# Expert 0's gathers: free of the last head group's stores, and taken head group by head group

## The chip, the cores and the metric

The kernel runs on one core of a Trainium2 chip. Its time is device microseconds (us) of one launch. The core's engines are named as the profile names them: PE multiplies matrices and also transposes them, DVE and ACT do elementwise work, POOL is a second elementwise engine that also issues the indirect transfers (gathers and scatters), and SP only issues plain transfers. Each engine takes its own instructions strictly in order; an instruction that has to wait holds up everything behind it on its engine. The transfers themselves run on 16 DMA engines shared by all issuers.

## What is computed

```python
# threshold attention: B=8, H=8, S=576, D=64
scores = q @ k.T / sqrt(D)
scores = where(scores >= max(scores) - tau, scores, -1e9)
attn   = softmax(scores)
x      = (attn @ v), laid out as 4608 tokens x 512      # a token's 8 heads side by side
# hash routing: E=8 experts, F=1024
e      = token_ids * 2654435761 % 8                       # depends on the ids alone
out[t] = relu(x[t] @ w1[e]) @ w2[e]
```

## The kernel before

**Attention.** The 64 (batch, head) problems are taken as 32 pairs: two neighbouring heads of one batch item. Pair `p` has `hp, b = divmod(p, 8)`, so the first eight pairs are head group 0 of all eight batch items, the next eight are group 1, and pairs 24 to 31 are group 3, the last. A head group is 128 columns of `x`. The loop runs over steps `n`, five to a pair (`p, s = divmod(n, 5)`), in an order of instructions that is written out by hand for every engine. In a step, PE makes scores (L235), DVE negates them and takes their maximum (L246, tile `ns`), POOL makes the threshold from the maximum (L253, tile `thr`), ACT exponentiates (L260), DVE applies the threshold to the exponentials (`mask`, L271, needs `thr`); two steps later PE transposes the weights (L282), ACT copies them (L303) and PE multiplies them with `v` (L313). The scores of a pair's first step are the only ones with a 64 row tile (`64*64` in the profile), so they mark where a pair begins.

**x goes through DRAM.** Two pairs late, in step `s == 0`, `put_xm` scales pair `p - 2`'s result (DVE, L352, tile `xm`) and SP stores it: one transfer of 256 KB (L358) and two of 16 KB (L363) into `x_scratch`, 576 rows of one head group's 128 columns. SP's queue also carries, in the same order as written, the loads of `k` (L190 to L192), `q` (L187) and `v` (L208, L212) for coming pairs, and four loads of 2 MB for the weights of the first two experts (L134 in pairs 20 and 24, L140 in pairs 22 and 26).

**Routing and expert 0's gathers.** Which tokens go to which expert is worked out during the first 23 pairs. Expert 0's tokens (up to 5 tiles of 128, `kt` = 0 to 4) are then fetched from `x_scratch` while the attention still runs: one gather is 128 rows of one head group (`fetch_0(kt, hp)`, issued on POOL by L119, into columns `128 hp` of buffer `xg_kt`). The 15 gathers of head groups 0 to 2 are spread over the last pairs; they stand in POOL's order between the `thr` instructions. The five of head group 3 follow after the loop, when pair 31 has been stored. Both sides name the whole of `x_scratch` to the scheduler of dependences: a gather names rows by an index, so it is taken to read all of it.

```python
 # L681  G0 = NS * ((HP - 1) * B + 1)                                    (= 125, the start of pair 25)
 # L682  early = [(kt, hp) for kt in range(KT) for hp in range(HP - 1)]
 # in the loop over n, in this order:
 s == 0: load_pair(p + 2), load_v(p + 1)        # SP: k, q, v
 s == 2, p in (22, 26): load_w2(...)            # SP: 2 MB
 s == 1: scale_k(p + 1)                         # POOL, L215
 s == 0, p >= 2: put_xm(p - 2)                  # DVE L352, SP L358, L363
 every s: mask(n - 1, j)                        # DVE L271
 if s in (2, 3) or s == 4 and n < G0 + 2 * NS:
     fetch_early(n)                             # POOL L119: next of `early`, if n > G0
```

So pairs 25 and 26 have three gathers each (s = 2, 3, 4), pairs 27 to 30 two (s = 2, 3), and the fifteenth is at n = 157 in pair 31.

**After the loop's last pair.** At n = 160 PE transposes what was gathered of tiles 0 to 3 (L614, 24 transposes) and, a little later, of tile 4; ACT copies the result into `xT_0`, and PE runs three quarters of expert 0's first layer (L640) while the last pairs finish. The experts follow in order of their load.

Of the kernel before, what the change touches and what calls it, by code (L numbers as in the profile page):

```python
# [20 lines left out]
def kernel(  # L21
# [12 lines left out]
    nc = tc.nc  # L34

    B, H, D, S = qT.shape
    N, DIN = out.shape
    E, _, F = w1.shape
    P = 128
    HP = H // 2  # L40
# [7 lines left out]
    NQ = 4  # L48
    TAIL = NQ * P
    NC = 5  # L50
    NS = 5
# [5 lines left out]
    KT, NB = 5, 19  # L57
# [21 lines left out]
    x_dram = nc.dram_tensor("x_scratch", (N, DIN), FP32, kind="Internal").ap()  # L79
    x_rows = x_dram.rearrange("n (h d) -> (n h) d", h=HP)  # L80
# [25 lines left out]
    gidx_0 = consts.tile([P, KT, HP], I32, name="gidx_0")  # L106
# [6 lines left out]
    xg_bufs = [consts.tile([P, DIN], FP32, name=f"xg_{i}") for i in range(KT)]  # L113
# [2 lines left out]
    w_tiles = {}  # L116

    def gather(src, dst, idx):
        nc.gpsimd.indirect_dma_start(  # L119
            out=dst, out_offset=None, in_=src,  # L120
            in_offset=bass.IndirectOffsetOnAxis(ap=idx, axis=0),
            bounds_check=src.shape[0] - 1, oob_is_err=False)

    def fetch_0(kt, hp):
        gather(x_rows, xg_bufs[kt][:, P * hp:P * hp + P], gidx_0[:, kt, hp:hp + 1])

    def expert_at(e):

# [15 lines left out]
    with tc.tile_pool(name="a_q", bufs=1) as a_q, \  # L144
# [59 lines left out]
        def load_v(p):  # L204
            hp, b = divmod(p, B)
            v_sb = v_bufs[p % 3]
            rows = v[b].rearrange("s h d -> s (h d)")[:, hp * P:hp * P + P]
            nc.sync.dma_start(out=v_sb[:, 0:4],  # L208
                              in_=rows[0:TAIL].rearrange("(c p) m -> p c m", p=P))
            for j in range(2):  # L210
                half = slice(64 * j, 64 * j + 64)
                nc.sync.dma_start(out=v_sb[half, 4, half], in_=rows[TAIL:S, half])  # L212
# [121 lines left out]
        def x_place(p):  # L334
            hp, b = divmod(p, B)
            return b * S, hp * P
# [10 lines left out]
        def put_xm(p):  # L347


            rec = recs.pop(p)  # L350
            xm = a_x.tile([P, NS, P], FP32, name="xm")
            nc.vector.tensor_tensor(  # L352
                out=xm[:].rearrange("p t (j d) -> p t j d", j=2),
                in0=av[:, :, 0:NS * D].rearrange("p j (t d) -> p t j d", t=NS),
                in1=rec[:].rearrange("p (t j) -> p t j", j=2)[:, :, :, None]
                .to_broadcast([P, NS, 2, D]), op=ALU.mult)
            r0, c0 = x_place(p)
            nc.sync.dma_start(  # L358
                out=x_dram[r0:r0 + TAIL, c0:c0 + P].rearrange("(t p) m -> p t m", p=P),
                in_=xm[:, 0:NQ])  # L360
            for j in range(2):
                cols = slice(D * j, D * j + D)
                nc.sync.dma_start(out=x_dram[r0 + TAIL:r0 + S, c0 + D * j:c0 + D * j + D],  # L363
                                  in_=xm[64 * j:64 * j + 64, NQ, cols])

        def route():

# [171 lines left out]
        def scatters():  # L539
# [20 lines left out]
            for _ in range(4):  # L560
# [11 lines left out]
                          in_=bass.AP(tensor=dataclasses.replace(token_ids.tensor,  # L572
                                                                 shape=[2 * N], dtype=I32),
                                      offset=0, ap=[[2 * NTC, P], [2, NTC], [1, 2]]))
# [94 lines left out]

        LAST = NS * NP  # L670
        G0 = NS * ((HP - 1) * B + 1)
        early = [(kt, hp) for kt in range(KT) for hp in range(HP - 1)]
        pieces, scatter_pieces = route(), scatters()
        h_pieces, held, LATE = early_h(), {}, (0, 6, 1, 7, 2, 3, 4, 5)
        assert FO == 8
# [12 lines left out]
        with tc.manual_schedule():  # L688
# [3 lines left out]
            for _ in range(17):  # L692
                nc.tensor.transpose(tr[:, 0, 0:P], ident[:], ident[:])
            nc.gpsimd.dma_start(out=tau_in[:],
                                in_=bass.AP(tensor=tau.tensor, offset=0, ap=[[0, P], [1, 1]]))
# [14 lines left out]
            for n in range(LAST + NS + 1):  # L710
                p, s = divmod(n, NS)
                m = n - 2
                if s == 0 and p + 2 < NP:
                    load_pair(p + 2)
                if s == 0 and p + 1 < NP:
                    load_v(p + 1)
                if s == 2 and p in (20, 24):
                    load_w1(p // 4 - 5)
                if s == 2 and p in (22, 26):
                    load_w2((p - 22) // 4)  # L720

                if (s == 3 and p > 0 or s == 2 and p in (9, 11, 13)) and not placed:
                    next(pieces)
                if s == 1 and 3 <= p < 2 + KT:
                    nc.sync.dma_start(out=xg_bufs[p - 2][:], in_=xg_bufs[0][:])

                if s == 1 and 2 + KT <= p < 2 + KT + N // DIN:
                    r0 = DIN * (p - 2 - KT)
                    nc.sync.dma_start(
                        out=x_dram[r0:r0 + DIN, DIN - P:].rearrange("(t p) m -> p t m", p=P),  # L730
                        in_=xg_bufs[0][:].rearrange("p (t m) -> p t m", m=P))
                q = p - 1
                if s == 1 and 0 <= q < NP:
                    add_eps(q)
                if s == (1 if p else 3) and p + 1 < NP:
                    scale_k(p + 1)
                if s == 2 and 0 <= q < NP:
                    nc.vector.reciprocal(recs[q][:], recs[q][:])
                if n == LAST + NS:
                    fill(2)  # L740
                if s == 0 and p >= 2:
                    turn_o()
                if n == LAST:
                    for k in (0, 2):
                        tr = ps_sc.tile([P, 2, 512], FP32, name="sc")
                        early_xT(tr, k, k + 2, 0, CO - 1)
                if s in (1, 2) and 0 <= q < NP and n != LAST + 1:
                    av_part(q, 0, ((0, 1, 2), (3, 4))[s - 1])
                if n < LAST and s in (1, 2):
                    negate(n, 0)  # L750
                    expo(n, 0)
                if s == 2 and 0 <= q < NP:
                    put_oT(0)
                if n > LAST:
                    fill(1)
                turned = 0 <= m < LAST
                if turned:
                    tr = turn_w(m, 0)
                    put_wT(m, 0, tr)
                if n == LAST:  # L760
                    put_xm(p - 2)
                    av_part(q, 0, (0, 1, 2))
                if n >= LAST:
                    fill(1)
                if n == LAST:
                    tr = ps_sc.tile([P, 2, 512], FP32, name="sc")
                    early_xT(tr, 4, 5, 0, CO - 1)
                if s in (3, 4) and 0 <= q < NP:
                    av_part(q, 1, ((0, 1, 2), (3, 4))[s - 3])
                if n < LAST and s not in (1, 2):  # L770
                    negate(n, 0)
                    expo(n, 0)
                if s == 0 and p > 0 and not placed:
                    next(pieces)
                if s == 0 and p >= 2 and n != LAST:
                    put_xm(p - 2)
                if s == 4 and 0 <= q < NP:
                    put_oT(1)
                if s in (3, 4) and turned:
                    tr = turn_w(m, 1)  # L780
                if n + 1 < LAST:
                    score(n + 1, 0)
                if s == 4 and turned:
                    put_wT(m, 1, tr)
                if n < LAST and heads(n) == 2:
                    negate(n, 1)
                    expo(n, 1)
                if s == 3 and turned:
                    put_wT(m, 1, tr)
                if n + 1 < LAST:  # L790
                    score(n + 1, 1)
                if s in (0, 1) and turned:
                    tr = turn_w(m, 1)
                    put_wT(m, 1, tr)
                if 0 < n <= LAST:
                    for j in range(heads(n - 1)):
                        mask(n - 1, j)
                if s < NS - 1 and placed:
                    next(scatter_pieces, None)
                if s in (2, 3) or s == 4 and n < G0 + 2 * NS:  # L800
                    fetch_early(n)
                if n == LAST:
                    fill(1)
            assert not early
            nc.vector.tensor_tensor(out=stok[:], in0=stok[:], in1=stok_odd[:], op=ALU.min)
            for h in range(4):
                rows, n = slice(32 * h, 32 * h + 32), (NB - h + 3) // 4
# [3 lines left out]
            for g in range(4):  # L811
                rows, n = slice(32 * g, 32 * g + 32), min(KT, NB - KT * g)
                nc.vector.tensor_copy(gidx_x[rows, 1:, 0:n], stok[rows, 1:, KT * g:KT * g + n])
            for _ in pieces:
                pass
            nc.vector.scalar_tensor_tensor(
                out=qidx[:], in0=stok[:], scalar=4.0,
# [7 lines left out]
    with tc.tile_pool(name="m_x", bufs=1) as m_x, \  # L825
# [534 lines left out]
        with tc.For_i(0, n_ov, 1) as it:  # L1360
# [5 lines left out]
                out=w1_sb[:],  # L1366
                in_=w1[bass.ds(ex, 1)].rearrange("o (c p) f -> p (o c) f", p=P))
            nc.gpsimd.dma_start(
                out=w2_sb[:],
                in_=w2[bass.ds(ex, 1)].rearrange("o (c p) d -> p (o c) d", p=P))  # L1370
# [53 lines left out]
```

## Time and profile before

| | us |
|---|---|
| median of 3 runs | 919.86 |
| lowest and highest of them | 915.38 and 920.58 |
| the profiled execution's own time | 919.78 |
| its span, first to last instruction | 918.1 |
| PE busy | 902.2 (98%) |
| DVE busy | 757.1 (82%) |
| POOL busy | 500.6 (55%) |
| granted TensorE clock | 0.998 |

A row of a timeline gives the start, the duration, the engine, the line and operation, what it writes and reads, and in square brackets the time that the engine was idle before it and what ended that idle time. `SPq` is SP's queue; its rows are the issuing of a transfer, not the transfer itself.

### The profile page before, as it was taken

To read this page: it belongs to the slowest core of one execution; us is meant where nothing else is said; L and a number is where in the kernel's file an instruction comes from. 1 tells how busy PE (TensorE), PEld (TensorE's weight loads), DVE (VectorE), ACT (ScalarE), POOL (GpSimd) and SP (SyncE) were. 2 spreads that over 40 slices of the span, in tenths; PEclk is the share of its full clock that TensorE was granted. 3 is DMA by queue.
4 is the path that set the end of the run, shared out by engine and by line. 5 is a ranking of instruction groups with operands and counts; after the bars stand their busy time and mean duration, and the time that the engine had idled before them with its cause. 6 is when DMAs were issued, how large, how long until landed. Compare 5 with 4: busy or idle time off the path is not lost.

```text
span 918.1 us, 21471 instructions
## 1 busy us (share of the span) xinstructions
PE 902.2 (98%) x7663; PEld 669.2 (73%) x7663; DVE 757.1 (82%) x1711; ACT 514.0 (56%) x848; POOL 500.6 (55%) x703
## 2 busy tenths in 40 slices
PE   8999999999999999999999999999999999999996
PEld 5666666666666666556668989889898988979885
DVE  8999999999999999989945796868778687776831
ACT  6888888888888898788922141422314132141321
POOL 4433443457667633545414388693959769391752
PEclk9999999999999999999999999999999999999999
DMA  7364463554546668654011546354343635431101
GB/s 179 92 148 119 111 153 96 136 127 109 126 95 142 182 165 223 186 125 104 16 30 53 159 167 211 118 165 156 85 159 130 208 115 151 157 91 30 32 23 55
DMA packets 114779, 113.15 MB, mean 123 GB/s; under 512 B 32475, under 2 KB 89315, under 8 KB 114672
## 3 DMA queue, kind: packets, MB, share of 16 engines
q1 hardware_dynamic: 105168, 92.64, 38.3%
q0 software_dynamic: 9072, 18.91, 6.6%
q8 instruction: 62, 1.02, 0.5%
q14 instruction: 45, 0.37, 0.1%
q10 hardware_dynamic: 432, 0.21, 0.1%
HBM read 81.99 MB, written 21.44 MB: 113 GB/s over the span
## 4 chain that ended last, share of the span: by engine, by line
PE 48%; POOL 27%; issue 15%; DVE 3%; ACT 2%; SPq 1%; DMA 1%; POOLq 1%; DVEq 0%; ACTq 0%
PE av L313 17%; POOL out_dram L1247 17%; PE sc L235 15%; PE tr L282 11%; POOL stok_odd L1232 8%; POOL xg L119 3%; PE sc L640 3%; PE av L282 2%; ACT w L260 1%; SPq L1277 1%; DVE w L271 1%; ACT wT_a L303 1%; DVE ns L246 1%; DMA k_sb<-in_k_dram 1%; POOLq L1247 0%
## 5 line engine op out<-in xcount | busy, mean ns | idle before, releaser
L260 ACT ACTIVATE w<-ns,nmx 128x576 f32<-128x576 f32 x288 | 220.3, 776 | 32.4 <-DVE ns L246 31.9
L271 DVE SCALAR_TENSOR_TENSOR w<-ns,thr,w 128x576 f32<-128x576 f32 x288 | 226.2, 817 | 4.2 <-POOL thr L253 4.2
L246 DVE TENSOR_SCALAR_CACHE_REDUCE ns<-sc 128x576 f32<-128x576 f32 x288 | 205.3, 745 | 6.7 <-PE sc L235 6.1
L1247 POOL DMA_INDIRECT out_dram<-o_q,qidx x127 | 147.7, 1163 | 113.4 <-DVE o_q L1238 80.1
L253 POOL TENSOR_SCALAR thr<-nmx,drop 128x2 f32<-128x2 f32 (+1 forms) x160 | 100.7, 630 | 165.8 <-DVE ns L246 157.8
L235 PE MATMUL sc<-k_sb,q 64*128 64x288 f32 (+1 forms) x1280 | 179.0, 422 | 1.4 <-DVE ns L246 1.0
L282 PEld LDWEIGHTS tr<-ident,w 64*128 64x128 f32 x2624 | 106.3, 138 | 92.5 <-ACT wT_a L303 28.8
L282 PE MATMUL tr<-ident,w 64*128 64x64 f32 x2624 | 138.9, 230 | 5.5 <-ACT wT_a L303 2.9
L235 PEld LDWEIGHTS sc<-k_sb,q 64*128 64x128 f32 (+1 forms) x1280 | 92.1, 177 | 24.8 <-DVE ns L246 12.2
L313 PE MATMUL av<-wT_a,v 128*64 128x320 f32 (+1 forms) x704 | 100.4, 418 | 0.2
L303 ACT COPY wT_a<-tr 128x512 f32<-128x512 f32 (+1 forms) x128 | 81.6, 638 | 22.4 <-PE tr L282 21.9
L303 ACT COPY wT_b<-tr 128x512 f32<-128x512 f32 (+1 forms) x128 | 81.2, 634 | 9.8 <-PE tr L282 8.1
L313 PE MATMUL av<-wT_b,v 128*64 128x256 f32 x640 | 83.2, 389 | 0.0
L1232 POOL COPY stok_odd<-stok 128x152 int32<-128x152 int32 x157 | 71.4, 455 | 0.6
L313 PEld LDWEIGHTS av<-wT_a,v 128*64 128x64 f32 x704 | 43.7, 136 | 29.0 <-DVE xm L352 0.5
L937 PE MATMUL bank<-h,w_sb 128*128 128x288 f32 (+4 forms) x248 | 62.0, 402 | 0.0
L937 PEld LDWEIGHTS bank<-h,w_sb 128*128 128x128 f32 x248 | 58.7, 290 | 0.5
L937 PE MATMUL sc<-h_s,w_s 128*128 128x288 f32 (+2 forms) x224 | 56.6, 406 | 0.0
L313 PEld LDWEIGHTS av<-wT_b,v 128*64 128x64 f32 x640 | 40.2, 136 | 18.8 <-issue 0.7
L961 ACT ACTIVATE h<-h 128x576 f32<-128x576 f32 (+1 forms) x42 | 29.0, 692 | 41.4 <-DVE h L864 36.3
L542 POOL DMA_INDIRECT slot_scratch<-tok,slot_i x36 | 46.6, 1294 | 8.5 <-issue 8.3
L119 POOL DMA_INDIRECT xg<-x_scratch,gidx_x x35 | 43.9, 1255 | 12.3 <-DVE xq L1269 5.3
(241 smaller groups left out, 1383.2 us busy)
## 6 DMA issues: line engine op xcount, KB each, us to landing
w_sb<-in_moe_w_dram SPq DMA_DIRECT2D x16, 2048.0 KB
q<-in_q_dram SPq DMA_DIRECT2D x62, 288.0 KB
v<-in_v_dram SPq DMA_DIRECT2D x32, 256.0 KB
x_scratch<-xm SPq DMA_DIRECT2D x32, 256.0 KB
xT<-xq SPq DMA_DIRECT2D x84, 80.0 KB
k_sb<-in_k_dram SPq DMA_DIRECT2D x31, 144.0 KB
k_sb<-in_k_dram SPq DMA_DIRECT2D x32, 112.0 KB
x_scratch<-xg SPq DMA_DIRECT2D x9, 256.0 KB
```

What stands on the lines that cost most here:

```text
L119: nc.gpsimd.indirect_dma_start(out=dst, out_offset=None, in_=src, in_offset=bass.IndirectOffsetOnAxis(ap=idx, axis=0), bounds_check=src.sh ...
L235: nc.tensor.matmul(sc[out_rows, i, 0:S2], lhsT=q_sb[rows, h, q0:q1], rhs=k_sb[rows, h], start=True, stop=True)
L246: nc.vector.tensor_scalar(out=ns[:].rearrange("p (i s) -> p i s", i=2), in0=sc[:, :, 0:S2], scalar1=-1.0, scalar2=None, op0=ALU.mult, op1= ...
L253: nc.gpsimd.tensor_scalar(out=thr[:, 0:j + 1], in0=stats[n][0][:, 0:j + 1], scalar1=drop[:], scalar2=None, op0=ALU.add)
L260: nc.scalar.activation(w, nss[n, j][:], AF.Exp, bias=stats[n][0][:, j:j + 1], scale=-1.0)
L271: nc.vector.scalar_tensor_tensor(out=w, in0=nss.pop((n, j))[:], scalar=stats[n][1][:, j:j + 1], in1=w, op0=ALU.is_le, op1=ALU.mult, accum_ ...
L282: nc.tensor.transpose(dst[:, r, 64 * c:64 * c + 64], src[rows, c0:c0 + P], ident[rows, rows])
L303: nc.scalar.copy(dst, tr[:, :, 0:64 * n_c].rearrange("p r (c q) -> p r c q", c=n_c))
L313: nc.tensor.matmul(av[64 * j:64 * j + 64, g, c0:c1], lhsT=v_sb[:, c, 64 * j:64 * j + 64], rhs=wT[g][:, i, c0:c1], start=(c == 0), stop=stop)
L937: nc.tensor.matmul(ps[:, i], lhsT=lhsT, rhs=y[:, c], start=start and c == 0, stop=c == len(lhsTs) - 1, skip_group_check=not start)
L1232: nc.gpsimd.tensor_copy(stok_odd[:], stok[:])
L1247: inst = nc.gpsimd.indirect_dma_start(out=rows[:, :], out_offset=bass.IndirectOffsetOnAxis(ap=idx, axis=0), in_=o_sb, in_offset=None, boun ...
```

## The change

It does three things. Stores of head group 3 and gathers of head groups 0 to 2 are declared to have no dependence on each other, which is so because they touch different columns; the gathers still depend on the stores of groups 0 to 2. The list of gathers is turned round: all five tiles of head group 0, then of group 1, then of group 2, instead of three groups of one tile after the other. And pair 26 has two gathers instead of three: the only one left at s = 4 is n = 129.

```diff
     def gather(src, dst, idx):
-        nc.gpsimd.indirect_dma_start(
+        return nc.gpsimd.indirect_dma_start(
...
+    def other_dims(inst, own, others):
+        inst = getattr(inst, "ins", inst)
+        tc.declare_no_dep(inst, group=others,
+                          reason="the last head pairs' dims are stored, dims of earlier ones gathered")
+        tc.add_to_no_dep_group(own, inst)
+
     def fetch_0(kt, hp):
-        gather(x_rows, xg_bufs[kt][:, P * hp:P * hp + P], gidx_0[:, kt, hp:hp + 1])
+        inst = gather(x_rows, xg_bufs[kt][:, P * hp:P * hp + P], gidx_0[:, kt, hp:hp + 1])
+        if hp < HP - 1:
+            other_dims(inst, "gathers", "stores")
...
             r0, c0 = x_place(p)
-            nc.sync.dma_start(
+            stores = [nc.sync.dma_start(
                 out=x_dram[r0:r0 + TAIL, c0:c0 + P].rearrange("(t p) m -> p t m", p=P),
-                in_=xm[:, 0:NQ])
+                in_=xm[:, 0:NQ])]
             for j in range(2):
                 cols = slice(D * j, D * j + D)
-                nc.sync.dma_start(out=x_dram[r0 + TAIL:r0 + S, c0 + D * j:c0 + D * j + D],
-                                  in_=xm[64 * j:64 * j + 64, NQ, cols])
+                stores.append(nc.sync.dma_start(
+                    out=x_dram[r0 + TAIL:r0 + S, c0 + D * j:c0 + D * j + D],
+                    in_=xm[64 * j:64 * j + 64, NQ, cols]))
+            if c0 == P * (HP - 1):
+                for inst in stores:
+                    other_dims(inst, "stores", "gathers")
...
-        early = [(kt, hp) for kt in range(KT) for hp in range(HP - 1)]
+        early = [(kt, hp) for hp in range(HP - 1) for kt in range(KT)]
...
-                if s in (2, 3) or s == 4 and n < G0 + 2 * NS:
+                if s in (2, 3) or n == G0 + 4:
                     fetch_early(n)
```

## The prediction

> **What bounds the kernel now.** I start with the page's first part, for which engine has no time to spare.
>
> ```profile
> span 918.1 us, 21471 instructions
> PE 902.2 (98%) x7663; PEld 669.2 (73%) x7663; DVE 757.1 (82%) x1711; ACT 514.0 (56%) x848; POOL 500.6 (55%) x703
> ```
>
> PE is busy nearly all the time, and the change takes no work from it. So a gain can come only from places where PE is made to wait or runs late, and only in the stretch that has the gathers. The timeline of PE shows that stretch, one row per pair: the first scores of pairs 26 to 31.
>
> ```profile
> 370.13 0.71 PE L235 MATMUL sc<-k_sb,q 64*64 64x288 f32 x8
> ...
> 384.46 0.71 PE L235 MATMUL sc<-k_sb,q 64*64 64x288 f32 x8
> ...
> 399.69 0.71 PE L235 MATMUL sc<-k_sb,q 64*64 64x288 f32 x8
> ...
> 416.20 0.72 PE L235 MATMUL sc<-k_sb,q 64*64 64x288 f32 x8
> ...
> 430.08 0.71 PE L235 MATMUL sc<-k_sb,q 64*64 64x288 f32 x8
> ...
> 443.98 0.71 PE L235 MATMUL sc<-k_sb,q 64*64 64x288 f32 x8
> ```
>
> The differences are 14.33, 15.23, 16.51, 13.88 and 13.90. Pair 25, which begins at 356.24, takes 13.89 too, so 13.89 is what a pair costs undisturbed, and pairs 26, 27 and 28 are 0.44, 1.34 and 2.62 too long: 4.40 us in all. Everything that this change can win is in there. DVE's timeline in the same stretch says what made them long.
>
> ```profile
> 369.88 0.82 DVE L271 SCALAR_TENSOR_TENSOR w<-ns,thr,w 128x576 f32<-128x576 f32 x1 [0.41 <-POOL thr L253]
> ...
> 385.04 0.82 DVE L271 SCALAR_TENSOR_TENSOR w<-ns,thr,w 128x576 f32<-128x576 f32 x1 [1.24 <-POOL thr L253]
> ...
> 401.61 0.82 DVE L271 SCALAR_TENSOR_TENSOR w<-ns,thr,w 128x576 f32<-128x576 f32 x1 [2.59 <-POOL thr L253]
> ```
>
> Three masks wait for their threshold, 4.24 us together, against 4.40 on PE: 0.41 answers to 0.44, 1.24 to 1.34, 2.59 to 2.62. POOL's timeline says why the thresholds were late: a gather stood in front of each.
>
> ```profile
> 368.36 1.13 POOL L119 DMA_INDIRECT xg<-x_scratch,gidx  x1 [3.94 <-DVE w L271]
> ...
> 383.56 1.10 POOL L119 DMA_INDIRECT xg<-x_scratch,gidx  x1 [4.82 <-DVE ns L246]
> ...
> 400.12 1.10 POOL L119 DMA_INDIRECT xg<-x_scratch,gidx  x1 [6.21 <-DMA x_scratch<-xm]
> ...
> 411.77 1.10 POOL L119 DMA_INDIRECT xg<-x_scratch,gidx  x1 [1.29 <-DMA x_scratch<-xm]
> ```
>
> The DVE named in the first two had long been done; all four wait for the newest store of x to land. Idle time on POOL minus the loss on DVE is 3.53, 3.58 and 3.62: a gather may hold POOL up for 3.6 us for nothing, since a threshold is ready that long before its mask, and every microsecond more is lost on DVE and PE. The fourth, 1.29, costs nothing, as it must. Last, SP's waits and its timeline show that the store was late in its turn.
>
> ```profile
> SPq L358 <- DMA xg<-x_scratch,gidx: 30.6, 5, 11.0
> ```
> ```profile
> 378.17 0.37 SPq L358 DMA_DIRECT2D x_scratch<-xm  x1
> ...
> 396.54 0.37 SPq L358 DMA_DIRECT2D x_scratch<-xm  x1
> ```
>
> Pair 24's result is ready on DVE at 372.86 and SP has issued the loads before it at 374.90, but the store goes at 378.17, when the third gather (begun 372.15) has landed. Pair 25's could go at 391.97 and goes at 396.54. Gather waits for store, store waits for gather, and both pass through busy DMA engines: a 2 MB load of w2 is issued at 380.60.
>
> **The change, part by part.** *The waits between gathers and group 3's stores go.* The first gather (n = 127) comes before any store of group 3: the last store ahead of it is pair 23's, of group 2, issued at 361.54. It still waits for that one, 3.94 us, so 0.41 on DVE and 0.44 on PE stay. The waits of 4.82, 6.21 and 1.29 are for stores of pairs 24, 25 and 26, all of group 3, and go: DVE gains 1.24 + 2.59 = 3.83, and PE, by its pairs, 1.34 + 2.62 = 3.96. What is late next in those pairs? Pairs 29 and 30 have two gathers each at the same places in POOL's order, and waited for no store; they take 13.88 and 13.90. So I put pairs 27 and 28 at 13.89.
>
> *SP no longer waits for gathers to land*: the stores of pairs 24, 25 and 26 leave earlier, pair 24's by 3.3 us (374.90 for 378.17), the other two by up to some 8, and so does what is queued behind them. The 2 MB load of w2 moves from 380.60 to about 377.4. The next loads of k (382.87) are no earlier, because they wait for PE to free their buffer; they run behind w2 as now. Nobody waits for w2 before the experts. I cost this at nothing; the cover is time: a load of k is issued some 18 us before POOL scales it (382.87 and 406.78 minus the 4 gained for pair 29's), and w2, issued at 380.60, had let SP's queue go on at 391.97. Were that cover gone, POOL would hold back a threshold, and PE lose one for one beyond 3.6.
>
> *A wait is added*: the scaling of k (L215), which sits on POOL ahead of the next threshold, now names its own three loads, which a gather's wait for later stores had covered. Queued behind it are `thr`, then the masks. It is the wait that the scalings of the earlier pairs have; the 31 scalings together idled 2.8 us, 0.09 each. Below nothing is excluded, since it is an added wait; above, five at 0.09 are 0.5, if all of it came out on PE. They have 3.6 us of cover, so I take 0.
>
> *The order of the gathers and the one moved.* POOL issues 15 gathers before and after, 1.0 to 1.65 each, all on POOL between thresholds. The gather at n = 134 goes, and one at n = 158 comes. There POOL has this room (timeline of POOL, around the last gather):
>
> ```profile
> 452.31 1.39 POOL L119 DMA_INDIRECT xg<-x_scratch,gidx  x1 [0.16 <-issue]
> 454.27 0.71 POOL L253 TENSOR_SCALAR thr<-nmx,drop 128x2 f32<-128x2 f32 x1 [0.57 <-DVE ns L246]
> 457.37 0.72 POOL L253 TENSOR_SCALAR thr<-nmx,drop 128x2 f32<-128x2 f32 x1 [2.38 <-DVE ns L246]
> ```
>
> A gather of 1.4 us goes into the idle 2.38 with 0.8 to spare: nothing. But the last gathers are needed sooner after their issue. Tile 3's last one moves to 452.3 and tile 4's to about 455.1, and PE takes them in here:
>
> ```profile
> 458.50 0.91 PE L614 MATMUL sc<-ident,xg 64*128 64x64 f32 x24
> ...
> 462.06 0.37 PE L614 MATMUL sc<-ident,xg 32*128 32x32 f32 x3
> ```
>
> That leaves 6.2 and 7.0 us from issue to use. The slowest landing that the stretch shows, from a gather's start to the store it let go, is 9.2 us (387.35 to 396.54), beside w2's load; another took 6.4 (401.75 to 408.19). At 452 SP's timeline has no load under way, and the last five gathers of the kernel, issued into the same quiet at 478.69 to 485.06, are all used by 489.16, the very last within 4.1. Cost 0 at 4.1; at the other end 9.2, a stall of 3.0. I take 0, by the nearer row.
>
> *Sum*, against the profiled execution: 919.78 - 3.96 = 915.8, of it 918.1 - 3.96 = 914.1 span. After 404 PE runs without a gap worth naming, and the experts' gathers and loads start from events on PE's path, so the gain should reach the end undiminished. The profiled execution and the median of the runs shown (919.86) are the same to 0.1, so 915.8 holds for the median as well. It is 0.43%. About 1% is what a measurement of this kernel can tell from no change: the three runs of before alone lie 5.2 us apart, so this forecast counts as within 1%.
>
> **A rule weighed against the rows.** The Trainium skill, "DMA: Bandwidth & Descriptors", section "Anatomy of one DMA — SWDGE (gpsimd) path", gives a transfer issued from GpSimd a nearly constant 2.0 us plus bytes over 436 GB/s. A gather of 64 KB would land about 2.2 us after its issue. By that, pair 24's store would leave at 375.4, pair 25's as soon as SP is free, 391.97, and with the landing times of the stores in the trace (5.4 and 3.6) the gathers behind them would wait about 2.0 and 1.7, under the 3.6 that are free: the removed waits would be worth nothing, and the time 919.8. The rows say 6.0 and 9.2 us from gather to released store, and a loss on DVE; they decide. Where the DMA engines are quieter than in this execution, though, the rule's case comes nearer, which is why my range leans upwards.
>
> **Rivals.** *The gain is partly there already or partly given back.* The run of 915.38 lies 4.4 below the others, the same 4.4 that these pairs lose; if the loss comes and goes with the state of the DMA queues, its removal moves the median less. Or a pair with gathers and freely moving stores costs more than 13.89: pairs 13 to 21, in which POOL issues the routing's scatters at the same places, take 13.89 to 14.47 by the same view of PE. At 0.4 each for the five pairs with moved gathers, 2 us come back: 917.8. Against it speak pairs 29 and 30. *More goes*: the first wait falls under its 3.6 too, 0.44 more, and the median falls on the low side of the scatter: 911 to 910. No row offers more. *Slower: the late gathers.* The transposes at n = 160 wait for the last gathers of tiles 3 and 4, PE stops, and all behind stop with it. Up to 6.2 us from issue it costs nothing, from there one for one, and it outweighs the gain from 6.2 + 4.0 = 10.2 us on; at 13 us the stall would be 6.8 and the time 919.8 - 4.0 + 6.8 = 922.6. Nothing in the trace landed that late. That the change *does not do what it says* I can exclude nearly: in the order of instructions with their waits, the stores of group 3 lose their waits for gathers, and gathers 4 to 15 theirs for stores.
>
> **Chances.** Forecast, 914 to 916.5: 0.64. Part given back, 916.5 to 920.5: 0.18. More, down to 911 and below: 0.10. Slower, above 920.5, through late gathers or a queue that I misjudge: 0.08. Range 911.0 to 920.5, which leaves out the last two. Faster by over 1% needs less than 910.7 (0.10); slower by over 1% needs more than 929.1, which takes gathers that land 20 us after issue or something unseen (0.05); within 1% the rest (0.85).
>
> **What would show it.** Right: pair 26 still 14.3, pairs 27 and 28 at 13.9; on POOL one gather with an idle time near 4 and no other above 1; the stores of pairs 24 and 25 right behind the loads of v; w2 issued near 377; the 24 transposes of L614 without a wait. Wrong: a mask that still waits for `thr` by more than 0.5 us after 371, a scaling of k with idle time before it, or a gap on PE at the first L614; and a pair of 14.3 among 27 to 31 would mean that a gather beside free stores has a price that I set to nothing.

## The result and the profile after

| | before | after |
|---|---|---|
| median of 13 runs each, us | 919.23 | 914.05 |
| lowest to highest | 915.38 to 921.04 | 913.57 to 914.76 |
| the profiled execution's own time | 919.78 | 914.5 |
| its span | 918.1 | 912.9 |

The measured ratio is 0.9964, with a 95% interval of 0.9952 to 0.9976, so 3.3 us (2.2 to 4.4). It is not the plain quotient of the two medians above, which lie 5.2 apart (0.9944); in the first group of experiments below, where both kernels ran on one chip, the medians lie 3.5 apart (917.27 and 913.78). The forecast was 915.8, a ratio of 0.9957. The second thing in the table is as large as the first: the runs of before are spread over 5.7 us, those of after over 1.2.

The page of after begins with these two lines; in the lines of after, the code lines are 8 or 12 higher than in before (L235 is now L243, L358 is L366).

```profile
span 912.9 us, 21463 instructions
...
PE 900.5 (99%) x7663; PEld 669.8 (73%) x7663; DVE 758.2 (83%) x1711; ACT 514.0 (56%) x848; POOL 503.3 (55%) x703
```

The same instructions on PE, less time. PE's timeline, the first scores of pairs 25 to 29:

```profile
355.25 0.72 PE L243 MATMUL sc<-k_sb,q 64*64 64x288 f32 x8
...
369.13 0.71 PE L243 MATMUL sc<-k_sb,q 64*64 64x288 f32 x8
...
383.03 0.72 PE L243 MATMUL sc<-k_sb,q 64*64 64x288 f32 x8
...
397.07 0.71 PE L243 MATMUL sc<-k_sb,q 64*64 64x288 f32 x8
...
410.96 0.71 PE L243 MATMUL sc<-k_sb,q 64*64 64x288 f32 x8
```

Pairs 25 to 28 take 13.88, 13.90, 14.04 and 13.89, where before had 13.89, 14.33, 15.23 and 16.51: 55.71 for 59.96, a gain of 4.25. From pair 29 to the end of the span both executions take the same, 501.90 and 501.94, so nothing is given back. The rest of the 5.2 us between the two spans, 0.99, lies before pair 25, where the instructions are the same; more on it below. POOL's timeline has the gathers of pairs 25 to 28, here the first of each pair:

```profile
365.98 1.13 POOL L119 DMA_INDIRECT xg<-x_scratch,gidx  x1 [2.56 <-DVE ns L254]
...
377.47 1.39 POOL L119 DMA_INDIRECT xg<-x_scratch,gidx  x1 [0.16 <-issue]
...
391.36 1.39 POOL L119 DMA_INDIRECT xg<-x_scratch,gidx  x1 [0.16 <-issue]
...
405.41 1.39 POOL L119 DMA_INDIRECT xg<-x_scratch,gidx  x1 [0.16 <-issue]
```

Only the first still waits. SP's timeline has the stores of pairs 24 and 25 and the load of w2 between them:

```profile
373.96 0.38 SPq L366 DMA_DIRECT2D x_scratch<-xm  x1
...
376.43 0.40 SPq L148 DMA_DIRECT2D w_sb<-in_moe_w_dram  x1
...
389.18 0.49 SPq L366 DMA_DIRECT2D x_scratch<-xm  x1
```

All three go 4 to 7 us earlier than before (1 us of it from ahead of pair 25), as soon as SP has issued what is ahead of them. And the list of DVE's waits from 355 to 460 us, which before was headed by 4.2 us of masks waiting for `thr`, has no mask left in it:

```profile
DVE ns L254 <- PE sc L243: 1.4, 7, 0.3
DVE rec L750 <- POOL rec L351: 0.7, 1, 0.7
```

### The profile page after: what moved, and what is told of

The parts are those of the page before. It is cut to its first block, busy times and chain, and to the rows that moved or that the text cites. A ratio compares the mean times of both kernels' runs of the same rounds, so it can differ in the third digit from the quotient of the medians.

```text
span 912.9 us, 21463 instructions
## 1 busy us (share of the span) xinstructions
PE 900.5 (99%) x7663; PEld 669.8 (73%) x7663; DVE 758.2 (83%) x1711; ACT 514.0 (56%) x848; POOL 503.3 (55%) x703
## 4 chain that ended last, share of the span: by engine, by line
PE 49%; POOL 28%; issue 15%; DVE 3%; ACT 2%; SPq 1%; DMA 1%; POOLq 1%; DVEq 0%; ACTq 0%
PE av L321 18%; POOL out_dram L1259 17%; PE sc L243 15%; PE tr L290 10%; POOL stok_odd L1244 7%; POOL xg L119 4%; PE sc L652 3%; PE av L290 1%; SPq L1289 1%; ACT w L268 1%; DMA k_sb<-in_k_dram 1%; DVE w L279 1%; DVE ns L254 1%; POOLq L1259 0%; PE sc L949 0%
## 5 line engine op out<-in xcount | busy, mean ns | idle before, releaser
L261 POOL TENSOR_SCALAR thr<-nmx,drop 128x2 f32<-128x2 f32 (+1 forms) x160 | 103.5, 647 | 169.3 <-DVE ns L254 163.9
L243 PE MATMUL sc<-k_sb,q 64*128 64x288 f32 (+1 forms) x1280 | 178.6, 423 | 1.0 <-DVE drop L716 0.7
L243 PEld LDWEIGHTS sc<-k_sb,q 64*128 64x128 f32 (+1 forms) x1280 | 92.8, 177 | 22.8 <-DVE ns L254 9.6
```

Source lines behind the costliest of these rows:

```text
L243: nc.tensor.matmul(sc[out_rows, i, 0:S2], lhsT=q_sb[rows, h, q0:q1], rhs=k_sb[rows, h], start=True, stop=True)
L261: nc.gpsimd.tensor_scalar(out=thr[:, 0:j + 1], in0=stats[n][0][:, 0:j + 1], scalar1=drop[:], scalar2=None, op0=ALU.add)
```

## Experiments

The experiments ran in three groups, each on one chip, and each group is compared within itself. The first group is the kernel after once more, the independence alone, order and pacing alone, and the load taken away. The second is two gathers in pair 26, both kernels with POOL held, and the loads beside the last gathers. The third is the kernel before once more and the three versions at the end. Every ratio is to the kernel before on the same chip.

**The kernel after once more.**

> The kernel after once more, on the same chip as the three others, for its ratio beside theirs and for a second profile. Theory (what the two traces differ in before pair 25, pair 1 and pairs 14 to 20, is chance of one execution and not the change): ratio 0.9945 to 0.9965, pairs 26 to 31 at 13.9 again, the stretch before pair 25 different by up to 2 us from the first profile of it. Rival (that stretch is part of the gain): again 13.89 for each of pairs 14 to 24, and the ratio of the kernel with only the dependence gone is worse than this one's by some 0.002.

Measured: 913.78, ratio 0.9963 (0.9951 to 0.9976); pairs 25 to 29 take 13.89, 13.89, 14.04, 13.89, 13.89. Pairs 15 to 21 are again at 13.89 each, which by itself is what the rival had said; whether that stretch belongs to the change needs both kernels. In the first profile of before six of these seven were above 14 (14.35, 14.38, 14.26, 13.89, 14.26, 14.08, 14.29). In both profiles of after, in a second profile of before itself and in all other kernels of the first and the last group, all seven are at 13.88 to 13.90; in the four kernels of the second group some of them are at 14.0 to 14.4 again. So it goes with the chip or the execution, and not with the kernel: before has it in one profile and not in the other. And pair 1 takes 14.15 in some executions and 15.32 in others of the same group. Both differ between kernels whose instructions up to there are the same, so the 0.99 us of the difference between the two spans is no gain of the change.

**The independence alone.**

```diff
# against the kernel after
-        early = [(kt, hp) for hp in range(HP - 1) for kt in range(KT)]
+        early = [(kt, hp) for kt in range(KT) for hp in range(HP - 1)]
-                if s in (2, 3) or n == G0 + 4:
+                if s in (2, 3) or s == 4 and n < G0 + 2 * NS:
```

> The kernel after, with the old order of the gathers (three head groups of one tile, then the next tile) and the old three gathers in pair 26: only the dependence between group 3's stores and the earlier groups' gathers is gone. Theory (the waits were the whole loss): all of the gain, ratio to before 0.994 to 0.9965, pairs 26 to 28 at 13.9 us each, no gather but the first with more than 1 us of idle time before it, same time as the kernel after within 1 us. Rival (order and pacing carry a part): less than half the gain, 917 us or more, with pair 26 over 14.2 because of its third gather.

Measured: 913.83, ratio 0.9968 (0.9957 to 0.9979), the same as the whole change. Pairs 26 to 28 take 13.91, 14.04 and 13.88. POOL's timeline has the first gather, and the third of pair 26:

```profile
365.81 1.49 POOL L119 DMA_INDIRECT xg<-x_scratch,gidx  x1 [2.93 <-DVE w L279]
...
382.88 1.37 POOL L119 DMA_INDIRECT xg<-x_scratch,gidx  x1 [0.17 <-issue]
```

The third gather costs nothing once it waits for nothing. So the dependence was enough by itself, and order and pacing add nothing to it that these runs can tell.

**Order and pacing alone.** The diff is the opposite one: before, with the new list and the new condition.

> The kernel before, with the new order of the gathers and two a pair from pair 26 on, but still dependent on every store. Theory: the gathers of pairs 26 to 28 wait 4 to 6 us for the newest store, over the 3.6 us that are free, so 1 to 2 us each are lost on DVE and PE and there is no gain: ratio 0.998 to 1.002, pairs 26 to 28 together about 3 to 4.4 us over 3 x 13.89. Rival (pacing carries it): ratio near 0.996, pairs 26 to 28 at 13.9.

Measured: 915.06, ratio 0.9974 (0.9962 to 0.9987), runs from 913.48 to 919.87. My expectation of no gain was wrong. The profiled execution, at 917.32, is the third longest of these 22 runs; it has pairs 26 to 28 at 15.81, 14.05 and 15.01, and two gathers and, behind them, two masks that wait:

```profile
368.73 1.13 POOL L119 DMA_INDIRECT xg<-x_scratch,gidx  x1 [5.42 <-DVE ns L246]
...
397.83 1.10 POOL L119 DMA_INDIRECT xg<-x_scratch,gidx  x1 [4.82 <-DVE ns L246]
```
```profile
370.26 0.82 DVE L271 SCALAR_TENSOR_TENSOR w<-ns,thr,w 128x576 f32<-128x576 f32 x1 [1.89 <-POOL thr L253]
...
399.31 0.82 DVE L271 SCALAR_TENSOR_TENSOR w<-ns,thr,w 128x576 f32<-128x576 f32 x1 [1.09 <-POOL thr L253]
```

The first mask stands behind the first gather, which waits for pair 23's store in every version. So the waits are still there; by their times, most executions of this kernel had less of them than this one, though that is argued and not seen.

**Two gathers in pair 26, and nothing else.**

```diff
# against the kernel before
-                if s in (2, 3) or s == 4 and n < G0 + 2 * NS:
+                if s in (2, 3) or n == G0 + 4:
```

> The kernel before, with nothing changed but the number of gathers in pair 26, two instead of three (one more in pair 31): old order, every dependence kept. The kernel with new order and two a pair, still dependent, won 0.0026 where I had expected nothing. Theory (the third gather of pair 26 is issued 3 to 6 us later than the second, holds pair 25's store that much longer, and the store holds the next gather): pacing is what won, ratio 0.9965 to 0.9985, median 914.5 to 916.5. Rival (the order by head groups won it): ratio 0.999 to 1.001.

Measured: 917.82, ratio 0.9986 (0.9974 to 0.9998), on a chip where before has 918.45. Between the two theories: less is won than I put down for pacing, and the interval barely leaves out 1, while the kernel before against itself comes to 1.0017 further below; so that pacing wins by itself is suggested and not shown. In its profile, at 916.32 the shortest of its twelve runs, the gathers of pairs 25, 26 and 27 do wait for stores, but none for more than 3.1 us, and no mask waits:

```profile
366.71 1.48 POOL L119 DMA_INDIRECT xg<-x_scratch,gidx  x1 [2.20 <-DVE ns L246]
...
380.45 1.10 POOL L119 DMA_INDIRECT xg<-x_scratch,gidx  x1 [1.87 <-DMA x_scratch<-xm]
...
395.85 1.35 POOL L119 DMA_INDIRECT xg<-x_scratch,gidx  x1 [3.10 <-DVE w L271]
```

Pair 25's store is issued at 390.88 in it and not at 396.54: the last gather ahead of that store is no longer the third one of pair 26. That is how pacing can win. But pairs 26 to 28 still take 14.36, 14.05 and 14.15 here, 0.89 us over, though no hold is above 3.6; this part the account of holds does not cover, and its cause is open. That the order of the list has a part of its own these two runs can't show or exclude.

**The load taken away instead of the dependence.**

```diff
# against the kernel before: the 2 MB of the second expert's w2 in pair 30
-                if s == 2 and p in (22, 26):
-                    load_w2((p - 22) // 4)
+                if s == 2 and p in (22, 30):
+                    load_w2(p // 30)
```

> The kernel before, with the 2 MB load of the second expert's w2 moved from pair 26 to pair 30; gathers and stores still wait for each other. Theory (the waits are long only because this load fills the DMA engines): gathers land in 3 to 5 us instead of 6 to 9, the waits of gathers in pairs 27 and 28 stay under 3.6 us, pairs 27 and 28 fall to 13.9 to 14.2, and 2.5 to 3.9 us are won without the change: ratio 0.996 to 0.9975. Rival (the loop of store and gather is slow in itself, whatever else is under way): pairs 27 and 28 still over 14.5, ratio 0.999 to 1.001.

Measured: 914.38, ratio 0.9970 (0.9958 to 0.9983), most of the change's gain with every dependence in place. The first gathers of pairs 25, 26 and 27 still wait, but 0.3, 0.8 and nothing over the free 3.6 us:

```profile
366.07 1.13 POOL L119 DMA_INDIRECT xg<-x_scratch,gidx  x1 [3.84 <-DVE w L271]
...
380.85 1.10 POOL L119 DMA_INDIRECT xg<-x_scratch,gidx  x1 [4.38 <-DVE ns L246]
...
394.12 1.47 POOL L119 DMA_INDIRECT xg<-x_scratch,gidx  x1 [2.92 <-DVE w L271]
```

Pairs 26 to 28 take 14.23, 14.80 and 13.89; pair 27 is over the 14.2 that I had put as its most. So it was the loop of waits and a load passing through it together: take either away and most of the loss is gone.

**The kernel before once more.**

> The kernel before itself, for a second profile of it and for the ratio of two equal kernels on this chip. Theory (its loss is made of waits whose length changes from execution to execution): ratio 1 within its interval; every gather with more than 3.6 us of idle time before it costs its excess on DVE, but the waits are others than in the first profile; pairs 26 to 28 together 1.5 to 7 us over 3 x 13.89. Rival (the loss is fixed): 0.4, 1.3 and 2.6 us again within 0.2.

Measured: 918.01, ratio 1.0017 (0.9999 to 1.0035). In this profile pairs 26 to 28 take 13.96, 14.59 and 17.37, 4.25 over. Again one can read the loss off POOL and DVE, but at other places:

```profile
380.96 1.10 POOL L119 DMA_INDIRECT xg<-x_scratch,gidx  x1 [4.17 <-DVE w L271]
...
398.40 1.10 POOL L119 DMA_INDIRECT xg<-x_scratch,gidx  x1 [7.09 <-DMA x_scratch<-xm]
```
```profile
382.44 0.82 DVE L271 SCALAR_TENSOR_TENSOR w<-ns,thr,w 128x576 f32<-128x576 f32 x1 [0.60 <-POOL thr L253]
...
399.89 0.82 DVE L271 SCALAR_TENSOR_TENSOR w<-ns,thr,w 128x576 f32<-128x576 f32 x1 [3.46 <-POOL thr L253]
```

4.17 minus 0.60 and 7.09 minus 3.46 are 3.57 and 3.63, the same 3.6. The waits change from execution to execution, the rule by which they cost does not. And 1.0017 for one kernel beside itself says that differences of this size come without any change.

**The rule by itself: POOL held by added operations.**

```diff
# against the kernel after, in fetch_early(n), ahead of the gather
+                if s == 2 and p in (27, 28, 29):
+                    for _ in range(10):          # 20 in the second kernel
+                        nc.gpsimd.tensor_scalar(out=spare[:], in0=spare[:], scalar1=1.0,
+                                                scalar2=None, op0=ALU.mult)   # spare: 128 x 120
```

> The kernel after, with ten small operations on a spare tile put on POOL ahead of one gather in each of pairs 27, 28 and 29: about 0.3 us each by the nearest rows, 3 us a pair. Theory (a hold of up to 3.6 us on POOL ahead of a gather is free, the rest is lost one for one): nothing lost, pairs 27 to 29 at 13.9 to 14.1, ratio as the kernel after. Rival (any hold costs, the cover is smaller): 1 to 3 us each, 917 to 923.

> As the kernel with ten operations, but with twenty ahead of the gather in each of the three pairs: about 6 us a pair. Theory: 6.0 minus 3.6 is 2.4 us lost in each of the three pairs (16.3 each), 7 us in all, about 921; if the twenty take another time than 6.0, the loss is that time minus 3.6 in each. The masks behind wait for their threshold by the same time. Rival (the loss of the kernel before came from busy DMA engines and not from POOL being held): no loss, 914.

Measured: 930.11, ratio 1.0118 (1.0094 to 1.0142), and 945.91, ratio 1.0299 (1.0276 to 1.0322). Neither number is near mine, because most of the operations take 0.51 us and not 0.3, some up to 1.0, and with about 0.08 us between two the ten hold POOL for 6.85 us and the twenty for 12.78. First POOL and then DVE, of the kernel with ten (the code lines of both are 2 higher than in after):

```profile
393.64 6.85 POOL L700 TENSOR_SCALAR spare<-spare 128x120 f32<-128x120 f32 x10
```
```profile
402.17 0.82 DVE L281 SCALAR_TENSOR_TENSOR w<-ns,thr,w 128x576 f32<-128x576 f32 x1 [3.29 <-POOL thr L263]
```

and of the kernel with twenty:

```profile
392.12 12.78 POOL L700 TENSOR_SCALAR spare<-spare 128x120 f32<-128x120 f32 x20
```
```profile
406.59 0.82 DVE L281 SCALAR_TENSOR_TENSOR w<-ns,thr,w 128x576 f32<-128x576 f32 x1 [9.22 <-POOL thr L263]
```

6.85 minus 3.29 and 12.78 minus 9.22 are both 3.56: 3.6 us are free, and what is above is lost one for one on DVE. PE loses more than DVE: pair 28 is 4.16 and 10.19 over, and pair 29 of the kernel with ten is 5.40 over (19.29). The trace shows what goes with it. These are stretches of 4 us of the kernel with ten (length, busy times of PE, of PE's weight loads, DVE, ACT and POOL, then the granted TensorE clock as a share of full speed, the share of the DMA engines, GB/s), and two rows of PE from the second of them:

```profile
399.00:403.00 4.00, 1.73 (x30) 0.99 (x28) 0.83 (x3) 2.09 (x4) 3.44 (x6) 1.00 0.66 157
403.00:407.00 4.00, 3.86 (x30) 2.68 (x32) 4.00 (x10) 1.91 (x3) 1.80 (x4) 0.57 0.94 210
407.00:411.00 4.00, 4.00 (x46) 2.40 (x42) 3.58 (x12) 3.06 (x6) 1.87 (x4) 1.00 0.14 38
```
```profile
403.14 0.64 PE L292 MATMUL tr<-ident,w 64*128 64x64 f32 x8 [2.42 <-DVE w L281]
403.52 2.29 PE L245 MATMUL sc<-k_sb,q 64*128 64x288 f32 x8
```

After PE has stood still for 2.42 us, the granted clock is 0.57 for 4 us, and eight matmuls of the scores take 2.29 us where they take 1.19 at full clock. After the second hold, in pair 29, the clock is at 0.50 from 421 to 427, longer than after the first. It does not follow from the length of the standstill alone: in the second profile of before PE stands still for 2.60 us ahead of 400.86, its clock stays at 1.00, and pair 28 loses 3.48 where DVE loses 3.46. What decides between the two these runs don't show. The ten missed the question of what a hold under 3.6 costs; before's fourth wait (1.29) and the ones above are the evidence that it is nothing.

Up to pair 27 the kernel with ten is the kernel after, and its first gather shows that the one wait which the change leaves can still cost:

```profile
369.38 1.13 POOL L121 DMA_INDIRECT xg<-x_scratch,gidx  x1 [4.73 <-DVE ns L256]
```
```profile
370.90 0.82 DVE L281 SCALAR_TENSOR_TENSOR w<-ns,thr,w 128x576 f32<-128x576 f32 x1 [1.20 <-POOL thr L263]
```

Pair 26 is at 15.12 in this execution.

**The slower rival's price: loads beside the last gathers.**

```diff
# against the kernel after: both loads of the second expert in pair 31
-                if s == 2 and p in (20, 24):
-                    load_w1(p // 4 - 5)
+                if s == 2 and p == 20 or s == 1 and p == 31:
+                    load_w1(p // 31)
-                if s == 2 and p in (22, 26):
-                    load_w2((p - 22) // 4)
+                if s == 2 and p == 22 or s == 1 and p == 31:
+                    load_w2(p // 31)
```

> The kernel after, with both 2 MB loads of the second expert (pairs 24 and 26) moved to the beginning of pair 31, so that they run while the last two early gathers are under way. It prices the slower rival. If landing under a load takes 6 to 9 us, as the trace of before showed, the first transposes of the gathered tiles (6.2 us after the issue of tile 3's last gather) wait, PE stops up to 3 us, and the time is 914 to 917 with a gap on PE ahead of the 24 transposes. If a gather gets through beside a load in under 6.2 us, no gap and 912.5 to 914: the rival has no price at all, and moving both loads wins the last few tenths of pairs 25 to 27.

Measured: 915.74, ratio 0.9967 (0.9954 to 0.9980), on the chip where before has 918.45. SP issues the two loads at 444.57 and 445.77. The table by stretches, with the columns as above, shows the DMA engines full just then:

```profile
448.00:452.00 4.00, 4.00 (x50) 2.56 (x48) 3.82 (x11) 3.81 (x6) 3.10 (x4) 1.00 1.02 412
452.00:456.00 4.00, 3.79 (x74) 2.78 (x72) 3.91 (x10) 3.58 (x8) 1.08 (x2) 1.00 1.01 360
```

POOL issues tile 3's and tile 4's last gathers into it, and PE takes in tiles 0 to 3 with no idle time ahead:

```profile
448.17 1.39 POOL L119 DMA_INDIRECT xg<-x_scratch,gidx  x1 [0.16 <-issue]
...
451.01 1.36 POOL L119 DMA_INDIRECT xg<-x_scratch,gidx  x1 [0.17 <-issue]
```
```profile
454.36 0.91 PE L626 MATMUL sc<-ident,xg 64*128 64x64 f32 x24
```

The last six of these 24 transposes are tile 3's, and the row ends at 455.27, so a gather of 64 KB lands within 7.1 us even beside two loads of 2 MB. The rival shows no price in this kernel. Pairs 26 and 27 are at 14.17 here with no wait that the trace shows, which I can't explain.

**Is there more to win?** Three versions of the kernel after: the load of w2 in pair 30; the first gather one step later; and both.

```diff
# the later start, against the kernel after
-            if n > G0 and early:
+            if n > G0 + 2 and early:
-                if s in (2, 3) or n == G0 + 4:
+                if s in (2, 3) or n in (G0 + 4, G0 + 9):
```

> The kernel after, with the 2 MB load of the second expert's w2 moved from pair 26 to pair 30. In the kernel before this move alone won 0.003. Theory (once no gather waits for a store of group 3, this load meets nobody that waits): nothing more, same as the kernel after within 0.001, pair 27 at 13.9 to 14.05. Rival (the load also slows pairs by itself): 1 us or more below the kernel after.

> The kernel after, with the first gather one step later (n = 128) and three gathers in pair 26. The first gather is the only one that still waits, for pair 23's store, 2.6 to 5.4 us in the profiles so far, and cost 0 to 1.9 us on DVE. One step is 2.8 us. Theory: its wait falls under 1 us, pair 26 is 13.9 in every execution, and the time is 0 to 0.8 us below the kernel after, whose ratio was 0.9963. Rival (three gathers in pair 26 cost): 0.5 us or more above the kernel after.

> Later first gather and late load of w2 together, the best version that the runs point to: 0 to 1 us below the kernel after, ratio 0.995 to 0.9963, pairs 25 to 31 all within 0.2 of 13.89.

Measured: 913.50, 913.50 and 913.57; ratios 0.9971 (0.9955 to 0.9987), 0.9966 (0.9951 to 0.9982) and 0.9968 (0.9952 to 0.9983). The load that won 0.0030 in before wins nothing here, as expected. The later start takes the last wait away, as POOL's timeline shows for its first gather, and pair 26 is at 13.89 with it:

```profile
366.16 1.13 POOL L119 DMA_INDIRECT xg<-x_scratch,gidx  x1 [0.94 <-DMA x_scratch<-xm]
```

None of the three differs from the change by more than the intervals can tell. What is left in the stretch is 0.15 us in pair 27.

## Why the prediction was right, point by point

**What bounded the stretch: right.** POOL held by a gather, 3.6 us of it free, the excess one for one on DVE, and on PE as long as its clock holds. It was read off three rows; in the further profiles idle time minus loss is 3.5 to 3.7 (5.42 less 1.89, 4.82 less 1.09, 4.17 less 0.60, 7.09 less 3.46), and 3.56 in both holds by added operations.

**The sum: right, with two terms off.** The forecast was 3.96 us for pairs 26 to 28, and the two profiles give 4.25. The term that was mis-sized is the first gather's: I let it wait its 3.94 us again and cost 0.44. It waited 2.56 and 3.42 in the two profiles of after, under the free 3.6, and pair 26 took 13.90 and 13.89: 0.43 more won, and the sign "pair 26 still 14.3" did not come. The wait follows from when SP comes to pair 23's store (5.30 us after the start of pair 25 in before, 3.85 in after) and how long the store takes to land. The 2 MB load of w1 is issued ahead of that store: in the other kernels with the first gather at its place the wait was 2.2 to 5.4 us with the load there, and 1.41 in the one execution where it had been moved to pair 31. That the load is the cause rests on this one. So the term is a matter of the execution and not fixed, as I had put it; in the six profiles with the independence, the first gather at its place and the load there, it stayed under the free 3.6 four times and went over twice, to 3.91 and 4.73. Against it stands 0.15 that I had not foreseen: pair 27 takes 14.04 and not 13.89, in after and in nearly every variant of it, whatever moves in or around it. In after the trace places it on ACT: the copy at 388.32 starts 0.82 us after the exponential ahead of it, where in pair 28 it is 0.68, and PE's next transposes are 0.15 later for it. Why is open. With these two terms the profiled execution of after comes out: 915.8 less 0.99 (the stretch before pair 25, no part of the change), less 0.43, plus 0.15 is 914.5.

**The costs set at nothing: right.** The added wait of the scaling of k does not appear among POOL's waits of after. The gather at n = 158 finds its place. w2's load went at 376.43; I had said 377.4 in an execution that began pair 25 0.99 later.

**The rule against the row: the row was right.** By the nearly constant landing time of the Trainium skill ("DMA: Bandwidth & Descriptors", "Anatomy of one DMA — SWDGE (gpsimd) path") the removed waits would have been worth nothing; they were worth the gain. The 6.0 and 9.2 us count from the start of the gather's issue; from its end, where I had set the rule's 2.2, they are 4.9 and 8.1, and the comparison stands. But the reason for the range's lean was right too: with the load of w2 moved away, waits shrink to 3.84, 4.38 and 2.92, and most of the gain is there without the change.

**The rivals.** Late gathers: refuted by the profile of their own experiment, at full DMA engines. *Partly there already*: it saw the cause of the scatter. Before's executions differ because its waits do, as its two profiles show; for the runs without a profile this is argued; the 62 runs of before beside the first group go from 913.5 to 920.7, while the kernel after's 16 beside them go from 913.1 to 915.3. So by these ranges the gain is 0 to 7 us, by execution, and the forecast from one profile was a draw from that; that the draw was a typical one was luck. The change's first effect is that the worst executions are gone.

**Not foreseen:** that pacing and order together, without the independence, would win anything. The prediction treated the moved gather as free, which it is once nothing waits; while the dependence stands, a gather late in a pair also delays the next store.

## What to carry to other kernels

When two queues wait for each other through a third resource (here store for gather, gather for store, both through the DMA engines), read off how long each may be late for nothing, and price only the excess; here a hold of 3.5 us cost nothing and one of 7 cost 3.5. A dependence that isn't real is worth removing for its spread as much as for its mean: compare the range of the runs, not only the medians. And before a gain read off one profile is believed, see from a second profile which of its terms are fixed and which are that execution's.

## What the runs showed of the hardware

- An operation on POOL over 128x120 takes 0.51 us (up to 1.0), with about 0.08 us to the next one of the same row; I had taken 0.3 from rows of other shapes.
- A gather of 128 rows of 512 bytes issued on POOL lands within 7.1 us while the DMA engines are fully busy with two loads of 2 MB on SP's queue.
- A pair of the attention loop can take 13.89 or 14.0 to 14.4 us, and pair 1 14.15 or 15.32, from execution to execution or from chip to chip, with no wait of a mask that the trace names.
- After PE had stood still for 2.42 us, the granted clock was 0.57 over the next 4 us; after 2.60 us in another execution it stayed at 1.00.
